# Pooled attention and a GELU MoE on one core: keys and values of batches 2 and 3 transposed through DRAM, and other chunks lent to VectorE

## Chip, cores and metric

The kernel runs on one core of a Trainium2 chip. The metric is the device time of one execution in microseconds (us); the time before is 948.67 us, the median of three runs (948.58 to 948.71).

## The reference

```python
# q: (4, 12288, 128)  kv: (4, 384, 32, 128)  w_sr: (128, 128)
# w_in: (128, 2048)   w_out: (2048, 128), all float32
kv_pool = kv.reshape(B, H // 4, 4, W // 4, 4, C).mean(axis=(2, 4))   # 96 x 8 = 768 keys a batch
k = v = kv_pool.reshape(B, -1, C) @ w_sr
s = (q @ k.transpose(0, 2, 1)) / np.sqrt(C)
a = softmax(s)
x = (a @ v).reshape(B * 12288, C)
h = x @ w_in
out = (h * sigmoid(1.702 * h)) @ w_out
```

Keys and values are the same matrix; the kernel needs it in two layouts, with channels along the partitions for the scores (kT) and with keys along the partitions for the weighted sum (v).

## The kernel before, in words

The 49152 tokens are 96 groups of 512. The work has two rounds of 48 groups, and in each round first the attention of all 48 groups, then their MoE. The unit is a chunk: 128 keys (6 a group, JC) or 128 hidden columns (16 a group, FCH) by 512 tokens, one bank of PSUM.

A **fill** writes up to three chunks into three banks with one matmul each (L350 for scores, L596 for hidden columns), and one ACTIVATE turns the three into exponentials (L352) or GELUs (L598) in SBUF. The two sets of three banks alternate. A **drain** consumes a chunk: L363, four matmuls of 129 columns for attention (the 129th sums the weights), or L606, one matmul of 512 columns into the output bank of the group. Two banks are left as accumulators (acc). When a group is finished VectorE (DVE) evacuates it: L386 and L389 divide and write x, L617 transposes the MoE's output into o_sb (three buffers), and four DMAs on SP's queue store it (L619). The last group is drained differently, by 64 matmuls of 128 columns (L634).

Some chunks skip ScalarE (ACT): DVE computes their exponential (early_exp, L426) or GELU (lent_gelu, L448) with a dozen elementwise instructions. Their matmuls are L415 and L409. Early chunks are the 24 of groups 48 to 51 (in the first MoE); rolling ones are the last chunk of listed attention groups (9 of them); lent ones are the last chunk of listed MoE groups (17, all in the second round). Rolling and lent results lie in three buffers (aside); raw, a buffer out of the queries' pool, holds a lent chunk's scaled input.

The order on every engine is written when the program is built. From L793 on, a planner keeps estimates of PE's, ACT's and DVE's time in units of one matmul; it places each fill two ahead of the drains, and puts drains and side jobs (extras, early steps) between fills as long as ACT's estimated end allows. background and background_moe (L527, L556) issue what goes with a group.

The keys of batches 2 and 3 are made during the first MoE. add_kv loads the 32 slices of kv with accumulating DMAs from POOL's queue, two per group, each pair behind a gate (a DVE memset that POOL's next memset waits for, L516); sum_kv (L176) adds two halves on DVE into pooled (96 rows by 4 x 128). Then come three side jobs on PE for each half a of a batch: transpose_pooled (L181: four transposes against an identity and a DVE copy into pT), make_k (L188: one matmul of 384 columns and a copy into kT) and make_v (L195: three matmuls of 128 columns and a copy into v). For batch 2 the adds begin at MoE group 2 and the sums stand at groups 12 and 14; for batch 3 at 24, 34 and 36 (L575 to L580).

Queries and, through x_bf, the attention's output already go through DRAM: put_away stores 3072 rows of x, bring_back loads them transposed with one DMA (L509), and load_qT does the same for 2048 queries (L215). All of these stand on SP's queue with the output stores.

Of the kernel before, what the change touches and what calls it, by code (L numbers as in the profile page):

```python
# [24 lines left out]
def kernel(  # L25
# [5 lines left out]
    r = 4  # L31
# [17 lines left out]
    q_flat = q.rearrange("b n c -> (b n) c")  # L49
    x_bf = nc.dram_tensor("x_bf", (B * N, C), BF, kind="Internal").ap()  # L50
    q_bf = nc.dram_tensor("q_bf", (B * N, C), BF, kind="Internal").ap()

    kv_r = kv.rearrange("b (ch p) (a w) c -> b a ch p (w c)", p=128, a=2)

# [43 lines left out]
    def acc_bf():  # L98
        return acc().bitcast(BF)
# [20 lines left out]
    def new_keys(b):  # L120
        kTs[b] = kvres.tile([128, J], BF, name="kT")

        vs[b] = kvres.tile([128, JC, C + 8], BF, name="v")
        nc.vector.memset(vs[b][:, :, C:C + 1], 1.0)

    def load_chunk(b, jc):
# [51 lines left out]
        pooled[b, a] = kvtmp.tile([Hp, 4, C], BF, name="pooled")  # L178
        nc.vector.tensor_tensor(pooled[b, a], t[:, 0], t[:, 1], ADD)

    def transpose_pooled(b, a):  # L181
        ps = acc_bf()[:, 0:h].rearrange("p (a b) -> p a b", a=4)
        for wp in range(4):
            nc.tensor.transpose(ps[:, wp, :], pooled[b, a][:, wp, :], ident[:Hp, :Hp])
        pTs[b, a] = kvtmp.tile([128, h], BF, name="pT")
        nc.vector.tensor_copy(pTs[b, a], ps.rearrange("p a b -> p (a b)"))

    def make_k(b, a):  # L188
        ps = acc()
        if a == 0:  # L190
            new_keys(b)
        nc.tensor.matmul(ps[:, :h], w_sr_sb, pTs[b, a], start=True, stop=True)  # L192
        nc.vector.tensor_copy(kTs[b][:, a * h:(a + 1) * h], ps[:, :h])

    def make_v(b, a):  # L195
        ps = acc()
        pT = pTs.pop((b, a))
        for k in range(K):
            nc.tensor.matmul(ps[:, k * C:(k + 1) * C], pT[:, k * 128:(k + 1) * 128], w_sr_sb,
                             start=True, stop=True)  # L200
        nc.vector.tensor_copy(vs[b][:, a * K:(a + 1) * K, 0:C], ps[:, :h].rearrange("p (k c) -> p k c", k=K))
        for jc in range(a * K, a * K + K):
            vs[b, jc] = True

# [123 lines left out]
        return K * len(free_frames())  # L328

    early = range(NG // R, NG // R + EARLY)  # L330
    rolling = [(i, JC - 1) for i in [10, *range(38, NG // R, 6), *range(57, 90, 6)]]
    lent = [(g, FCH - 1) for g in range(52, 94) if g % 5 in (2, 4)]
    aside = agpool.tile([128, K, 512], BF, name="aside")

    def weights(c):
        if c[0] == "a" and c[1] in early:
            return ag[:, (c[1] - early[0]) * JC + c[2], :]
        if c[0] == "a" and c[1:] in rolling:
            return aside[:, rolling.index(c[1:]) % K, :]
        if c[0] == "m" and c[1:] in lent:  # L340
            return aside[:, (len(rolling) + lent.index(c[1:])) % K, :]
        return ag[:, slot_of[c], :]


# [56 lines left out]
    COEFFS = (1.0000001192092896, -0.6931469440460205, 0.24022120237350464, -0.05550713464617729, 0.009675541892647743, -0.001327647129073739)  # L401

    def early_fill(i, jc):
        nonlocal steps, raw
        ps = acc()
        if (i, jc) in lent:
            if raw is None:
                raw = qpool.tile([128, 1, SG], BF, name="qT")[:, 0, 0:2 * G].bitcast(F32)
# [8 lines left out]
        early_step()  # L417

    def early_step():
# [59 lines left out]
    raw = None  # L479
    made, used = {}, []  # L480
    steps, early_todo = None, [c for c in rolling if c[0] < early[0]]
    early_todo += [(i, jc) for i in early for jc in range(JC)]
    early_todo += [c for c in rolling if c[0] > early[-1]] + lent

    def early_fits(p, i, jc):
        if (i, jc) in rolling:
            group = seq[p][1][0][0] if seq[p][0] == "a" else seq[p][1][0][0] // (NG // R) * (NG // R) + NG // R - 1
            return (i // GB, jc) in vs and (i in turned or i // 4 in qTs and i // 4 - 1 <= group // 4 and i >= 4 * QS) and len(used) > rolling.index((i, jc)) - K
        if (i, jc) in lent:
            return seq[p][0] == "m" and seq[p][1][0][0] >= i - 2 and len(used) > len(rolling) + lent.index((i, jc)) - K  # L490
        return low and min(slot_of.values()) >= low and (2, JC - 1) in vs

    def early_waits(t):
# [26 lines left out]
        nc.vector.memset(one, 0.0)  # L520
        nc.gpsimd.memset(one, 0.0)  # L521

    TURN = {6: 3, 7: 4, 8: 5, 20: 6, 21: 7, 22: 8, 25: 9, 32: 10, 35: 11, 40: 12}
    CAST = {0: [5], 13: [6], 14: [7], 15: [8], 16: [9], 26: [10, 11], 27: [12]}
    CAST_MOE = {20: 13, 21: 14, 22: 15, 23: 16, 33: 17, 34: 18, 35: 19, 36: 20, 37: 21, 38: 22, 39: 23}

    def background(i):  # L527

        first_round = i < GB * 2
        s = TURN.get(i, NS) if first_round else i // 4 + 3 if i % 4 == 0 else NS  # L530
        if s < NS:
            load_qT(s)
        if i in CAST:
            gate()
            for s in CAST[i]:
                cast_q(s)
        if i in (10, 12):
            gate()
            for jc in range(i % 10 * 3 // 2, i % 10 * 3 // 2 + 3):
                load_chunk(1, jc)  # L540
        if 0 <= i - 16 < JC:
            extras.append((key_and_value, 1, i - 16))
        if 0 <= i - 15 < JC:
            extras.append((pool_chunk, 1, i - 15))
        if i in (28, 33, 38):
            put_away(0, (i - 28) // 5)
        if i in (31, 36, 41):
            bring_back(0, (i - 31) // 5)
        if i == 28:
            gate()  # L550
            nc.gpsimd.dma_start(out=w_in_sb, in_=moe_w_in)
        if i == 29:
            gate()
            nc.gpsimd.dma_start(out=w_out_sb, in_=moe_w_out.rearrange("(o p) c -> p o c", p=128))

    def background_moe(g):  # L556

        n, g = divmod(g, 4 * XS)
        m, odd = divmod(g - 9, 2)
        m += FIRST  # L560
        if n == 0 and FIRST <= m < RT // PART:
            (bring_back if odd else put_away)(n, m)
        g += n * 4 * XS
        nonlocal low
        if g == 12:
            low = EARLY * JC
            order[:] = [f for f in order if f >= low // K]
        if g in CAST_MOE:
            gate()
            cast_q(CAST_MOE[g])  # L570
        if g in (41, 42):
            load_qT(g - 28)
        if g == 43:
            background(early[0])
        for b, lo in ((2, 2), (3, 24)):  # L575
            if lo <= g < lo + 8:
                gate()
                add_kv(b, g - lo)
            if g in (lo + 10, lo + 12):
                use_kv(b, (g - lo - 10) // 2)  # L580

    def use_kv(b, a):
        nonlocal extra_at
        sum_kv(b, a)
        on_dve(3.5)
        extra_at = max(extra_at, dve + 1.5)
        extras.extend([(transpose_pooled, b, a), (make_k, b, a), (make_v, b, a)])

    extras = []

# [120 lines left out]
    def prepare(p):  # L711
# [3 lines left out]
        for i, jc in part:  # L715
# [30 lines left out]
    FIXED, CHUNK, SWITCH, HANDOVER, EVACUATE = 0.295, 1.978, 6.0, 1.0, 4.5  # L746
    COST = {pool_chunk: (1.9, 2.6), key_chunk: (0.3, 2.4), value_chunk: (0.3, 2.4),
            transpose_q: (1.05, 4.2), early_fill: (1.0, 5.5), key_and_value: (0.55, 3.5),
            transpose_pooled: (0.9, 3.6), make_k: (0.8, 3.2), make_v: (0.8, 3.7)}
# [8 lines left out]
    def on_dve(cost):  # L758
        nonlocal dve
        dve = max(dve, now + 1.0) + cost  # L760
# [36 lines left out]
    for n in range(len(seq)):  # L797
        fill(n + 2)
        jobs(n + 3)
        while True:  # L800
# [13 lines left out]
            if f:  # L814
                now = max(now, bank) + COST[f][0]
                f(*args)
                free[last_acc] = dve + 1.0 if f is early_fill else copied(f)
                if f in (transpose_pooled, make_k, make_v):
                    on_dve(2.5)
                extra_at = max(now + PAUSE, dve + 1.5 if f in (transpose_pooled, make_k, make_v) else 0.0)  # L820
# [72 lines left out]
```

## Time and profile before

| | before |
|---|---|
| median of the runs | 948.67 us |
| span of the profiled execution | 946.7 us (2.0 under the median) |
| PE busy | 933.9 us, 6200 matmuls on record, 6314 weight loads |
| ACT busy | 933.5 us |
| DVE busy | 575.1 us, 61% |
| POOL busy | 66.5 us |
| granted TensorE clock | 1.000 |
| first fill of the first MoE | about 140 us |
| first fill of the second MoE | about 603 us |

The span is the time from the first to the last instruction of one execution under the hardware profiler. PE is TensorE's matmul row and PEld its weight loads, which overlap the matmul before. Busy time counts an engine as busy while any of its instructions is open; since matmuls and ACTIVATEs overlap their neighbours, a share of 99% does not say which engine the others wait for. The times from one matmul's or load's start to the next say more, and they are used below.

### The profile page before, as it was taken

What the parts mean: (1) busy time and instruction counts of PE and PEld (TensorE: products, weight loads), DVE (VectorE), ACT (ScalarE), POOL (GpSimd) and SP (SyncE); (2) the same over time, 40 slices, a digit from 0 to 9 for tenths busy, and PEclk for the clock granted to TensorE, in tenths of its full rate; (3) what the DMA queues carried; (4) which work ended last, traced back from release to release, by engine and by line L of the source; (5) the groups of instructions that cost most, each with busy time, mean ns of one, the idle gap of its engine ahead of it and who ended that gap; (6) DMA issues with size and microseconds to landing.
All of it is one profiled execution on the core that took longest, in us unless ns stands there. A gap on an engine that the chain in (4) does not pass through costs nothing.

```text
span 946.7 us, 15374 instructions
## 1 busy us (share of the span) xinstructions
PE 933.9 (99%) x6200; PEld 502.5 (53%) x6314; DVE 575.1 (61%) x1091; ACT 933.5 (99%) x709; POOL 66.5 (7%) x115
## 2 busy tenths in 40 slices
PE   8999999999999999999999999999999999999998
PEld 4677776444444444444446777744444444444444
DVE  5753653011678776667765765376767766777651
ACT  6999999999999999999999999999999999999998
POOL 3101001330000232000000000000000000000000
PEclk9999999999999999999999999999999999999999
DMA  9997943999867799865335683552222222222222
GB/s 210 195 207 168 181 92 52 130 163 170 164 117 114 119 147 119 127 99 87 56 58 105 138 170 84 119 123 42 36 39 40 38 41 34 44 34 45 34 45 46
DMA packets 372856, 95.46 MB, mean 101 GB/s; under 512 B 346720, under 2 KB 370400, under 8 KB 372320
## 3 DMA queue, kind: packets, MB, share of 16 engines
q1 hardware_dynamic: 344000, 62.36, 36.9%
q0 software_dynamic: 28512, 31.99, 22.3%
q8 instruction: 49, 0.80, 0.3%
q14 instruction: 23, 0.19, 0.1%
q10 hardware_dynamic: 272, 0.13, 0.0%
HBM read 52.49 MB, written 48.76 MB: 107 GB/s over the span
## 4 chain that ended last, share of the span: by engine, by line
PE 97%; ACT 1%; DMA 1%; issue 1%; DVE 0%; POOL 0%; POOLq 0%
PE banks L606 35%; PE banks L596 34%; PE banks L363 14%; PE banks L350 12%; ACT ag L352 1%; PE banks L415 1%; DMA x<-in_kv_dram 1%; PE banks L139 0%; PE banks L409 0%; PE banks L634 0%; PE banks L236 0%; POOL x L222 0%; PE banks L161 0%; PE banks L294 0%; PE banks L192 0%
## 5 line engine op out<-in xcount | busy, mean ns | idle before, releaser
L598 ACT ACTIVATE ag<-banks 128x1536 bf16<-128x1536 f32 (+1 forms) x509 | 681.1, 1489 | 0.0
L596 PE MATMUL banks<-x,w_in_sb 128*128 128x512 bf16 x1476 | 405.8, 379 | 1.7
L606 PE MATMUL banks<-ag,w_out_sb 128*128 128x512 bf16 x1477 | 402.6, 379 | 1.7
L352 ACT ACTIVATE ag<-banks 128x1536 bf16<-128x1536 f32 (+2 forms) x192 | 245.6, 1421 | 3.5 <-PE banks L236 2.3
L606 PEld LDWEIGHTS <-w_out_sb 128*128 128x128 bf16 x1520 | 148.3, 98 | 177.2 <-issue 0.2
L596 PEld LDWEIGHTS <-w_in_sb 128*128 128x128 bf16 x1519 | 147.1, 98 | 171.3 <-issue 0.7
L617 DVE STREAM_TRANSPOSE o_sb<-banks 128x512 f32<-128x512 f32 x95 | 68.1, 717 | 171.4 <-PE banks L606 166.9
L363 PEld LDWEIGHTS <-ag 128*128 128x128 bf16 x2268 | 145.5, 98 | 44.6 <-issue 0.3
L363 PE MATMUL banks<-v,ag 128*128 128x129 bf16 x2268 | 163.0, 220 | 0.2
L350 PE MATMUL banks<-qT,kT 128*128 128x512 bf16 x498 | 145.0, 379 | 3.5 <-ACT ag L352 0.5
L442 DVE SCALAR_TENSOR_TENSOR ea<-ea,eb 128x512 f32<-128x512 f32 x132 | 90.4, 685 | 3.7 <-DVE ea L442 0.7
L386 DVE RECIPROCAL rec<-banks 128x3 f32<-128x3 f32 x124 | 22.3, 180 | 85.3 <-PE banks L363 84.9
L389 DVE TENSOR_TENSOR x<-banks,rec 128x384 bf16<-128x384 f32 x124 | 69.1, 557 | 4.3
L350 PEld LDWEIGHTS <-kT 128*128 128x128 bf16 x543 | 45.8, 98 | 25.9 <-issue 2.0
L473 DVE RECIPROCAL eb<-ea 128x256 f32<-128x256 f32 x34 | 57.6, 1724 | 0.5
L466 DVE SCALAR_TENSOR_TENSOR ea<-ea,eb 128x512 f32<-128x512 f32 x68 | 46.5, 683 | 1.9
L173 POOL DMA_DIRECT2D kvs<-in_kv_dram x32 | 40.4, 1323 | 19.3 <-DMA kvs<-in_kv_dram 17.1
L431 DVE TENSOR_SCALAR ea<-banks 128x512 f32<-128x512 f32 x33 | 22.8, 692 | 29.6 <-PE banks L415 29.2
L521 POOL MEMSET gate_tile<- 1x1 f32 x38 | 3.4, 89 | 325.8 <-DVE gate_tile L520 325.8
L453 DVE TENSOR_SCALAR qT<-banks 128x512 f32<-128x512 f32 x17 | 11.8, 692 | 20.7 <-PE banks L409 20.6
L437 DVE SCALAR_TENSOR_TENSOR eb<-eb,ea 128x512 f32<-128x512 f32 x33 | 22.8, 691 | 0.9
L444 DVE SCALAR_TENSOR_TENSOR ag<-ea,ee 128x512 bf16<-128x512 f32 x24 | 16.6, 691 | 1.2
(83 smaller groups left out, 286.3 us busy)
## 6 DMA issues: line engine op xcount, KB each, us to landing
out_dram<-o_sb SPq DMA_DIRECT2D x380, 64.0 KB, 2.0
kvs<-in_kv_dram POOLq DMA_DIRECT2D x32, 384.0 KB, 6.3
q_bf<-in_q_dram POOLq DMA_DIRECT2D x21, 512.0 KB, 6.6
x_bf<-x SPq DMA_DIRECT2D x13, 768.0 KB, 5.6
x<-in_kv_dram POOLq DMA_DIRECT2D x11, 512.0 KB, 10.4
x_bf<-x SPq DMA_DIRECT2D x6, 384.0 KB, 4.6
x<-in_q_dram POOLq DMA_DIRECT2D x5, 256.0 KB, 15.3
x<-in_kv_dram SPq DMA_DIRECT2D x1, 1024.0 KB, 5.0
```

Of the source, the lines that this page charges most:

```text
L173: nc.gpsimd.dma_start(out=kv_sums[b][:, i2], in_=kv_p[b, i, w, :, i2], **({"accum_op": ADD} if n else {}))
L350: nc.tensor.matmul(ps[:, k, :], kTs[i // GB][:, jc * 128:(jc + 1) * 128], rhs, start=True, stop=True)
L352: nc.scalar.activation(place([("a",) + c for c in chunks]), ps, AF.Exp, scale=scale)
L363: nc.tensor.matmul(av_of[u][:, k * (C + 1):(k + 1) * (C + 1)], weights(("a", i, jc))[:, o:o + T], vs[i // GB][:, jc, 0:C + 1], start=(jc = ...
L389: nc.vector.tensor_tensor(to, ps[:, :, 0:C], rec.unsqueeze(2).broadcast_to([128, TS, C]), MUL)
L442: nc.vector.scalar_tensor_tensor(a, a, COEFFS[k], b, ADD, MUL)
L466: nc.vector.scalar_tensor_tensor(a, a, COEFFS[k], b, ADD, MUL)
L473: nc.vector.reciprocal(b[:, m:m + 256], a[:, m:m + 256])
L596: nc.tensor.matmul(ps[:, k, :], w_in_sb[:, fc * 128:(fc + 1) * 128], x[:, g % (4 * XS) * G:(g % (4 * XS) + 1) * G], start=True, stop=True)
L598: nc.scalar.activation(place([("m",) + c for c in chunks]), ps, AF.Gelu_apprx_sigmoid)
L606: nc.tensor.matmul(o_of[g], w_out_sb[:, fc, :], weights(("m", g, fc)), start=(fc == 0), stop=(fc == FCH - 1))
L617: nc.vector.transpose(o_sb, o_of.pop(g))
```

## The change

Four things change together.

- The side jobs transpose_pooled and make_v are gone. pooled is stored to DRAM (pool_bf) and loaded back transposed into pT by a DMA; make_k is as it was; then kT's half is stored to DRAM (k_bf) and three transposing DMAs write the three chunks of v. All of these DMAs stand on SP's queue. v's rows become 144 columns wide instead of 136.
- Each step has its own group. Batch 2's adds begin at group 0 instead of 2, batch 3's still at 24. For half a, counted from the first group of the adds: the sum and its store at 9 + a, the transposing load at 11 + a, make_k at 13 + a, the store of kT at 15 + a, the loads of v at 17 + a.
- 22 GELU chunks go to DVE instead of 17, three of them (groups 5, 7, 8) in the first MoE, and 10 rolling exponentials instead of 9, at other groups. The aside buffers are handed out in one common order (turn).
- raw is taken before the first MoE (at attention group 40) and again for the second, so the load of query set 12 moves from group 40 to 42.

```diff
-        vs[b] = kvres.tile([128, JC, C + 8], BF, name="v")
+        vs[b] = kvres.tile([128, JC, C + 16], BF, name="v")
...
-    def transpose_pooled(b, a):
...
+    def put_pooled(b, a):
+        nc.sync.dma_start(out=pool_bf[b, a].rearrange("w h c -> h w c"), in_=pooled[b, a])
+
+    def turn_pooled(b, a):
+        pTs[b, a] = kvtmp.tile([128, 1, h], BF, name="pT")
+        nc.sync.dma_start_transpose(out=pTs[b, a], in_=pool_bf[b, a].rearrange("w h c -> (w h) c"))
+
+    def put_k(b, a):
+        jc = slice(a * K, a * K + K)
+        nc.sync.dma_start(out=k_bf[b, jc].rearrange("j c t -> c j t"),
+                          in_=kTs[b][:, a * h:(a + 1) * h].rearrange("c (j t) -> c j t", t=128))
+
+    def turn_k(b, a):
+        for jc in range(a * K, a * K + K):
+            nc.sync.dma_start_transpose(out=vs[b][:, jc:jc + 1, 0:C], in_=k_bf[b, jc])
...
-    def make_v(b, a):
...
-    rolling = [(i, JC - 1) for i in [10, *range(38, NG // R, 6), *range(57, 90, 6)]]
-    lent = [(g, FCH - 1) for g in range(52, 94) if g % 5 in (2, 4)]
+    rolling = [(i, JC - 1) for i in (11, 29, 39, 42, 53, 55, 61, 73, 76, 89)]
+    lent = [(g, FCH - 1) for g in (5, 7, 8, 52, 54, 56, 57, 61, 62, 65, 68, 70, 72, 75, 77, 79, 81, 83, 86, 89, 92, 94)]
...
-    TURN = {6: 3, 7: 4, 8: 5, 20: 6, 21: 7, 22: 8, 25: 9, 32: 10, 35: 11, 40: 12}
+    TURN = {6: 3, 7: 4, 8: 5, 20: 6, 21: 7, 22: 8, 25: 9, 32: 10, 35: 11, 42: 12}
...
+        if i == 40:
+            new_raw()
...
         if g == 43:
+            raw = None
             background(early[0])
-        for b, lo in ((2, 2), (3, 24)):
+        for b, lo in ((2, 0), (3, 24)):
             if lo <= g < lo + 8:
                 gate()
                 add_kv(b, g - lo)
-            if g in (lo + 10, lo + 12):
-                use_kv(b, (g - lo - 10) // 2)
...
+            for a in range(2):
+                step = g - lo - 9 - a
+                if step == 0:
+                    sum_kv(b, a)
+                    on_dve(3.5)
+                    put_pooled(b, a)
+                if step == 2:
+                    turn_pooled(b, a)
+                if step == 4:
+                    extras.append((make_k, b, a))
+                if step == 6:
+                    put_k(b, a)
+                if step == 8:
+                    turn_k(b, a)
```

In the built programs PE has 16 transposes (L184), 12 value matmuls (L199) and their weight loads less and is otherwise equal in number; DVE has 8 copies less and the instructions of five GELUs and one exponential more; SP has 24 DMAs more; ACT has 499 GELUs of 1536 columns instead of 501, one more of 512, and one exponential of 1536 columns turned into one of 1024.

More of the change, by code (lines that the diff above doesn't have):

```diff
@@ L51 @@
     q_bf = nc.dram_tensor("q_bf", (B * N, C), BF, kind="Internal").ap()
+    pool_bf = nc.dram_tensor("pool_bf", (B, 2, r, Hp, C), BF, kind="Internal").ap()
+    k_bf = nc.dram_tensor("k_bf", (B, JC, C, 128), BF, kind="Internal").ap()
     kv_r = kv.rearrange("b (ch p) (a w) c -> b a ch p (w c)", p=128, a=2)
@@ L179, in sum_kv @@
         nc.vector.tensor_tensor(pooled[b, a], t[:, 0], t[:, 1], ADD)
-    def transpose_pooled(b, a):
[L182 to L186, printed above, removed]
+    def put_pooled(b, a):
[10 more added lines that the diff above has]
+            nc.sync.dma_start_transpose(out=vs[b][:, jc:jc + 1, 0:C], in_=k_bf[b, jc])
     def make_k(b, a):
@@ L191, in make_k @@
             new_keys(b)
-        nc.tensor.matmul(ps[:, :h], w_sr_sb, pTs[b, a], start=True, stop=True)
+        nc.tensor.matmul(ps[:, :h], w_sr_sb, pTs.pop((b, a))[:, 0, :], start=True, stop=True)
         nc.vector.tensor_copy(kTs[b][:, a * h:(a + 1) * h], ps[:, :h])
-    def make_v(b, a):
[L196 to L201, printed above, removed]
         for jc in range(a * K, a * K + K):
@@ L330 @@
     early = range(NG // R, NG // R + EARLY)
-    rolling = [(i, JC - 1) for i in [10, *range(38, NG // R, 6), *range(57, 90, 6)]]
-    lent = [(g, FCH - 1) for g in range(52, 94) if g % 5 in (2, 4)]
+    rolling = [(i, JC - 1) for i in (11, 29, 39, 42, 53, 55, 61, 73, 76, 89)]
+    lent = [(g, FCH - 1) for g in (5, 7, 8, 52, 54, 56, 57, 61, 62, 65, 68, 70, 72, 75, 77, 79, 81, 83, 86, 89, 92, 94)]
+    turn = [("a",) + c for c in rolling if c[0] < early[0]] + [("m",) + c for c in lent if c[0] < early[0]]
+    turn += [("a",) + c for c in rolling if c[0] > early[-1]] + [("m",) + c for c in lent if c[0] > early[-1]]
     aside = agpool.tile([128, K, 512], BF, name="aside")
@@ L337, in weights @@
             return ag[:, (c[1] - early[0]) * JC + c[2], :]
[L338 to L341, printed above, removed]
+        if c in turn:
+            return aside[:, turn.index(c) % K, :]
         return ag[:, slot_of[c], :]
@@ L403, in early_fill @@
     def early_fill(i, jc):
-        nonlocal steps, raw
+        nonlocal steps
         ps = acc()
@@ L407, in early_fill @@
             if raw is None:
-                raw = qpool.tile([128, 1, SG], BF, name="qT")[:, 0, 0:2 * G].bitcast(F32)
+                new_raw()
             nc.tensor.matmul(ps, w_in_sb[:, jc * 128:(jc + 1) * 128],
@@ L417, in early_fill, with new_raw @@
         early_step()
+    def new_raw():
+        nonlocal raw
+        raw = qpool.tile([128, 1, SG], BF, name="qT")[:, 0, 0:2 * G].bitcast(F32)
     def early_step():
@@ L481 @@
     steps, early_todo = None, [c for c in rolling if c[0] < early[0]]
+    early_todo += [c for c in lent if c[0] < early[0]]
     early_todo += [(i, jc) for i in early for jc in range(JC)]
-    early_todo += [c for c in rolling if c[0] > early[-1]] + lent
+    early_todo += [c for c in rolling + lent if c[0] > early[-1]]
     def early_fits(p, i, jc):
@@ L487, in early_fits @@
             group = seq[p][1][0][0] if seq[p][0] == "a" else seq[p][1][0][0] // (NG // R) * (NG // R) + NG // R - 1
-            return (i // GB, jc) in vs and (i in turned or i // 4 in qTs and i // 4 - 1 <= group // 4 and i >= 4 * QS) and len(used) > rolling.index((i, jc)) - K
+            return (i // GB, jc) in vs and (i in turned or i // 4 in qTs and i // 4 - 1 <= group // 4 and i >= 4 * QS) and len(used) > turn.index(("a", i, jc)) - K
         if (i, jc) in lent:
-            return seq[p][0] == "m" and seq[p][1][0][0] >= i - 2 and len(used) > len(rolling) + lent.index((i, jc)) - K
+            return seq[p][0] == "m" and seq[p][1][0][0] >= i - 2 and len(used) > turn.index(("m", i, jc)) - K
         return low and min(slot_of.values()) >= low and (2, JC - 1) in vs
@@ L548, in background @@
             bring_back(0, (i - 31) // 5)
+        if i == 40:
+            new_raw()
         if i == 28:
@@ L563, in background_moe @@
         g += n * 4 * XS
-        nonlocal low
+        nonlocal low, raw
         if g == 12:
@@ L578, in background_moe @@
                 add_kv(b, g - lo)
-            if g in (lo + 10, lo + 12):
-                use_kv(b, (g - lo - 10) // 2)
[L582 to L587, printed above, removed]
+            for a in range(2):
[12 more added lines that the diff above has]
+                    turn_k(b, a)
     extras = []
@@ L748 @@
             transpose_q: (1.05, 4.2), early_fill: (1.0, 5.5), key_and_value: (0.55, 3.5),
-            transpose_pooled: (0.9, 3.6), make_k: (0.8, 3.2), make_v: (0.8, 3.7)}
+            make_k: (0.8, 3.2)}
     COPY = {pool_chunk: 1.5, key_chunk: 1.5, value_chunk: 1.5, key_and_value: 2.8, transpose_q: 3.2}
@@ L817 @@
                 free[last_acc] = dve + 1.0 if f is early_fill else copied(f)
-                if f in (transpose_pooled, make_k, make_v):
+                if f is make_k:
                     on_dve(2.5)
-                extra_at = max(now + PAUSE, dve + 1.5 if f in (transpose_pooled, make_k, make_v) else 0.0)
+                extra_at = max(now + PAUSE, dve + 1.5 if f is make_k else 0.0)
                 if f is early_fill:
```

## The prediction

> **What bounds the kernel now.** I read four views: the busy times, the chain that ended last, the groups of matmuls with their weight loads, and the timeline around the removed instructions. The page, first parts 1 and 4, then groups:
>
> ```profile
> PE 933.9 (99%) x6200; PEld 502.5 (53%) x6314; DVE 575.1 (61%) x1091; ACT 933.5 (99%) x709; POOL 66.5 (7%) x115
> ...
> PE 97%; ACT 1%; DMA 1%; issue 1%; DVE 0%; POOL 0%; POOLq 0%
> ...
> L598 ACT ACTIVATE ag<-banks 128x1536 bf16<-128x1536 f32 (+1 forms) x509 | 681.1, 1489 | 0.0
> L596 PE MATMUL banks<-x,w_in_sb 128*128 128x512 bf16 x1476 | 405.8, 379 | 1.7
> L606 PE MATMUL banks<-ag,w_out_sb 128*128 128x512 bf16 x1477 | 402.6, 379 | 1.7
> ...
> L606 PEld LDWEIGHTS <-w_out_sb 128*128 128x128 bf16 x1520 | 148.3, 98 | 177.2 <-issue 0.2
> L596 PEld LDWEIGHTS <-w_in_sb 128*128 128x128 bf16 x1519 | 147.1, 98 | 171.3 <-issue 0.7
> ```
>
> PE and ACT are both at 99%, so which of them is the bound has to be decided. The chain says PE (97%). The groups show a trap: L606 has 1520 weight loads but 1477 matmuls, so 43 matmul records are missing, and a missing one looks like a gap of 0.216 us. I therefore take the steps from one weight load's start to the next, less the width of the matmul between. PE's idle time is then 10.4 us in all: 9.0 in the first 60 us, and only 1.4 in the 883 us after them. ACT is not so tight: half of the 499 steps between GELUs of 1536 columns take 1331 ns, the mean is 1344, and each longer step (1347, 1387) ends in an ACTIVATE that starts 414 ns after the last matmul of its fill, the shortest such distance in the stretch I listed. There ACT waits for PE. **PE is the bound**, and ACT has about 0.2 us to spare in 20.
>
> Next, the removed instructions in the timeline (start, length, engine, line):
>
> ```profile
> 228.85 0.40 PEld L184 LDWEIGHTS <-pooled 96*128 96x128 bf16 x4
> 229.06 0.34 PE L184 MATMUL banks<-ident,pooled 96*128 96x96 bf16 x4
> ...
> 229.23 0.81 PE L596 MATMUL banks<-x,w_in_sb 128*128 128x512 bf16 x3
> ...
> 231.56 0.33 PE L199 MATMUL banks<-w_sr_sb,pT 128*128 128x128 bf16 x3
> 231.67 0.37 PEld L596 LDWEIGHTS <-w_in_sb 128*128 128x128 bf16 x3
> 231.72 0.81 PE L596 MATMUL banks<-x,w_in_sb 128*128 128x512 bf16 x3
> ```
>
> From 229.06 to the next fill at 229.23 the four transposes cost 0.17 us; the three value matmuls 0.16 to 0.17 (231.56 to 231.72). Nothing waits around them.
>
> **The change, part by part.**
>
> *Removed from PE:* 16 transposes at 42.5 ns apart and 12 value matmuls at 56: 0.68 + 0.67 = **-1.35 us**. All of it lies on the saturated engine. make_k's four matmuls stay.
>
> *GELU and exponentials moved to DVE.* A lent chunk's matmul only moves from L596 to L409 (or L350 to L415) and its drain stays, so PE's work is unchanged. ACT loses two 1536-column GELUs net of one new 512-column one, and a 1536-column exponential becomes a 1024-column one. By start-to-start steps (1331, 904 and 477 ns) that is 2 x 1.331 - 0.477 + 0.427 = 2.6 us, on an engine that waits for PE anyway: I cost it at nothing. It keeps ACT ahead of the lighter PE. Counting chunks filled and not yet drained in the built order, before never has under 8 between 15 and 930 us, and after has as many or more from 90 to 915 us (up to 9 more): PE always has a drain to run.
>
> DVE gains 5 GELUs of 11.05 us (sum of its 15 rows from L453 to L475, 3.45 of it the two reciprocals) and one exponential of 6.1, and loses 8 copies (4 x 0.36 + 4 x 0.56): 55.3 + 6.1 - 3.7 = 57.7, so 61% becomes 67%. Three GELUs fall in groups 3 to 9, where the trace has DVE idle 5.97 us of each 6.7. What can become late is an output's evacuation (L617) behind a 1.72 us reciprocal; the next group drains into the other accumulator bank and needs the first one a group (some 7 us) later. If that cover fails, at most 1.7 us a time. In before, gaps of 38 to 108 ns follow 7 of the 50 matmuls made for DVE (0.55 us together): six more cost 0.07.
>
> *Transposing through DRAM.* SP gains 24 DMAs: 4 puts of pooled, 4 turns of 384 rows, 4 puts of keys, 12 turns of 128 rows. No such small turn is in the trace; the nearest rows:
>
> ```profile
> out_dram<-o_sb SPq DMA_DIRECT2D x380, 64.0 KB, 2.0
> kvs<-in_kv_dram POOLq DMA_DIRECT2D x32, 384.0 KB, 6.3
> ...
> qT<-q_bf SPq DMA_TRANSPOSE x21, 4.2
> ...
> x<-x_bf SPq DMA_TRANSPOSE x16, 7.4
> ```
>
> The 21 turns of 2048 rows land in 3.8 to 8.3 us, those of 3072 in 5.0 to 17.5; issuing holds SP at least 1.64 and 2.95. By the two shortest, 1.2 us per 1024 rows, a 384-row turn lands in about 1.9 (an estimate); the far end is 8.3. I take 2 to 4, since it is smaller than the nearest row.
>
> Three waits are new. (1) make_k waits for the turned keys. For each batch the second turn writes the one pT buffer, so on SP it waits for the first make_k on PE. In the built order the second make_k stands 6.85 us of PE work later in batch 2 (6.6 in batch 3); less the first matmul and the issue, about **6.1 us** remain for landing. At 2 to 4 us that costs nothing; at 8.3 it costs 2.2 us in each of two places. (2) Behind that waiting turn on SP stand the next group's four output stores, held some 7 us; o_sb has three buffers, so an evacuation needs them three groups later, and the next x turns are for groups tens of us ahead. (3) The sums now come at groups 9 and 10 instead of 12 and 14, and batch 2's adds two groups earlier, at 0 to 7, on a POOL queue that had idled 64.8 us before them and has nothing else queued until group 20. The last pair then lands near 203 us (issued about 195, landing 5.6 to 6.7 us in that stretch before) and the sum stands near 205; if late by 2 us, DVE's next work (a GELU whose chunk is drained 10 us later, and an evacuation) takes it. The second sum also waits until the first put has left the one pooled buffer: 2.0 to 12.2 us by the rows (12.2: x's store at 207.6, beside the adds that now end earlier), with a group between. The value turns are issued at groups 17 and 18; the first early drain that reads them is at 22. The query turn moved from group 40 to 42 is first read about 100 us later.
>
> *The tail.* The last fill is now one chunk. The three matmuls that wait for group 94's evacuation (L634 into the held bank) stand 0.94 us after the last L606's start (two steps of 0.216 and nine of 0.056); in the trace that evacuation ends 1.13 us after it (938.12 to 938.53 + 0.72). **+0.2 us.** The first 835 matmuls, 67 us, stand as before, so the start's 9 us of idle stay.
>
> *Sum:* -1.35 + 0.2 + 0.07 = -1.1 us. The span of 946.7 becomes 945.6; the median of the runs lies 2.0 above the span, so 948.67 becomes **947.6**.
>
> Two rules of the Trainium skill speak against this. "VectorE: DVE Perf Modes", The three transpose paths, gives 390 ns for a 128x128 transpose on TensorE and 1309 through the DMA crossbar, and its rules say to use TensorE where PSUM will do. By it a 384-row turn is three of these, an estimate of 3.9 us, still under the 6.1 above: the same sum. The rows here show why the slower path may pay: PE's next transpose starts 42 ns later, yet PE has no other idle time to put it in. "Perfetto Trace Analysis", Identifying the Most-Contended Engine, calls matmul busy time a poor measure and uses weight-load busy time: 53% here, so PE would look half free and ACT the bound, and the gain would be ACT's 2.6. The load-to-load steps disagree; this case follows the steps.
>
> **Rivals.**
> - *ACT is the bound* and its 2.6 us come off: 946.1. For: 99% busy, half the steps at their shortest. Against: 1.4 us of PE idle in 883. Chance 0.09.
> - *PE waits for the turned keys* at make_k, at the second half of each batch, if a turn lands over 6.1 us after issue. Two landings of 8 to 8.5 us give +3.8 to +4.8: 951.4 to 952.4, slower than before by over 0.2% from about 7.7 on. For: rows up to 8.3 and 17.5, casts on the same DMA engines for batch 3. Also for: the page's DMA row shows 0.9 and 0.8 of the engines busy around batch 2's turns, 0.6 around batch 3's. Against: a fifth to an eighth of those rows' size, and batch 2's adds are over earlier. Chance 0.11.
> - *DVE is late* with evacuations or a sum, one or two reciprocals' worth seen by PE: +0.4 to +1.8, 948.0 to 949.4. Chance 0.08.
> - *Forecast:* 946.8 to 948.2, chance 0.72.
>
> The range takes the forecast and the late DVE, 946.8 to 949.4, leaving out 0.20. About 0.2% (1.9 us) is what a measurement can tell from no change; the forecast lies within it. Faster 0.09, same 0.80, slower 0.11.
>
> **What would show it.** Right: no L184 and L199 rows; PE idle by load steps still about 1.4 us after 60 us; ACT's mean step longer than 1344 or unchanged while its work is 2.6 us less; no wait of PE at make_k's L192. Wrong: a wait there for a DMA, L617 waiting for DVE with PE gaps behind it, or ACT steps at 1331 with PE gaps between fills.

## The result, and the profile after

The changed kernel takes **947.22 us** (median of 20 runs, 947.08 to 947.95), the kernel before 948.57 (20 runs beside them, 948.33 to 948.75): 1.35 us less, a ratio of 0.9987 (0.9981 to 0.9993). The forecast was 1.1 us less. The difference lies under the 0.2% that the prediction took as measurable; its interval leaves out 1. The span of the profiled execution falls from 946.7 to 945.4 us.

The page of the changed kernel, in the rows that answer to those of before (busy time, count; then the shares of the chain that ended last; then groups with busy time, mean ns and the idle time before them). Lines have moved: L612 is the fill (L596 before), L622 the drain (L606), L614 the GELU (L598), L633 the evacuation (L617), L203 make_k's matmul (L192), L650 the last group's drain (L634). The kernels of the experiments have numbers of their own, a few lines off.

```profile
PE 938.4 (99%) x6286; PEld 501.3 (53%) x6286; DVE 630.5 (67%) x1168; ACT 931.0 (98%) x708; POOL 66.8 (7%) x115
...
PE 97%; ACT 1%; DMA 1%; DVE 0%; issue 0%; POOL 0%; POOLq 0%
...
L614 ACT ACTIVATE ag<-banks 128x1536 bf16<-128x1536 f32 (+1 forms) x508 | 679.1, 1470 | 0.0
L612 PE MATMUL banks<-x,w_in_sb 128*128 128x512 bf16 x1514 | 409.6, 379 | 0.0
L622 PE MATMUL banks<-ag,w_out_sb 128*128 128x512 bf16 x1498 | 405.2, 379 | 0.0
...
L622 PEld LDWEIGHTS <-w_out_sb 128*128 128x128 bf16 x1520 | 148.6, 98 | 178.6 <-issue 0.2
```

Three things are to be read here, and one isn't. PE has 28 weight loads fewer (6314 to 6286): the 16 transposes and 12 value matmuls. ACT has 2.5 us less and DVE 55.4 more (57.7 was worked out). What isn't to be read is that PE is busy 4.5 us longer: this profile lost fewer matmul records (L612 has 1514 for its 1514 weight loads, where the fill before had 1476 for 1519), and busy time counts the records that are there.

The steps between weight loads, read as in the prediction, are not touched by that. PE's idle time after the first 60 us is 1.40 us before and 1.73 after (first 60 us: 8.96 and 8.91); its work is 1.35 us less; its last matmul ends at 943.40 and at 942.33. The level of 1.40 hangs on the width taken for a matmul: some 0.2 ns more for each makes it about 0.7. The differences between kernels, on which what follows rests, move by 0.01 with it. So -1.35 + 0.33 - 0.05 = -1.07, which is the whole shift of PE's end. The remaining 0.2 of the span lie behind it, where the last stores land (3.28 us from PE's end to the span's end before, 3.09 after).

The new idle time is in few places: 194 ns before the first fill of the first MoE (139.84), 134 ns before the fill at 405.72, 185 ns in all behind matmuls made for DVE (550 before), and 253 ns at the end. The first two are waits for ACT: the ACTIVATEs that free the banks end at 139.79 and 405.67. The last of them, in the timeline of the changed kernel (start, length, engine, line; the bracket is the idle time before and what ended it):

```profile
937.91 0.38 PE L622 MATMUL banks<-aside,w_out_sb 128*128 128x512 bf16 x1
...
938.13 0.33 PE L650 MATMUL banks<-w_out_sb,ag 128*128 128x128 bf16 x3
...
938.33 0.72 DVE L633 STREAM_TRANSPOSE o_sb<-banks 128x512 f32<-128x512 f32 x1 [5.83 <-PE banks L622]
938.51 0.86 PE L650 MATMUL banks<-w_out_sb,ag 128*128 128x128 bf16 x8
939.10 0.15 PEld L650 LDWEIGHTS <-ag 128*128 128x128 bf16 x2 [0.21 <-issue]
```

Group 94's evacuation ends at 938.33 + 0.72 = 939.05. PE has run the matmuls that don't need its bank by then (the last fill is one chunk now), and the next load starts at 939.10. That is the tail term of the prediction: 0.2 forecast, 0.25 measured.

The transfers of the changed kernel, from its DMA rows (issues, KB each, median us from issue to landing):

```profile
pool_bf<-pooled SPq DMA_DIRECT2D x4, 96.0 KB, 4.5
k_bf<-kT SPq DMA_DIRECT2D x4, 96.0 KB, 2.1
...
v<-k_bf SPq DMA_TRANSPOSE x12, 2.6
...
pT<-pool_bf SPq DMA_TRANSPOSE x4, 5.8
```

And batch 3's second turn in the timeline:

```profile
405.21 0.33 PE L203 MATMUL banks<-pT,w_sr_sb 128*128 128x384 bf16 x1
...
405.56 4.78 SPq L188 DMA_TRANSPOSE pT<-pool_bf  x1
...
411.98 0.33 PE L203 MATMUL banks<-pT,w_sr_sb 128*128 128x384 bf16 x1
```

The turn is issued when the first make_k has read pT, holds SP's queue for 4.78 us and lands 5.9 us after its issue, at 411.5: half a microsecond before the matmul that reads it. The four landings are 5.6, 2.2, 6.1 and 5.9 us; the prediction took 2 to 4. Nothing waited, but the cover was nearly used up.

### The profile page after: what moved, and what is told of

It reads as the page before. It is cut to its first block, busy times and chain, and to the rows that moved or that the text cites. A ratio compares the mean times of both kernels' runs of the same rounds, so it can differ in the third digit from the quotient of the medians.

```text
span 945.4 us, 15529 instructions
## 1 busy us (share of the span) xinstructions
PE 938.4 (99%) x6286; PEld 501.3 (53%) x6286; DVE 630.5 (67%) x1168; ACT 931.0 (98%) x708; POOL 66.8 (7%) x115
## 4 chain that ended last, share of the span: by engine, by line
PE 97%; ACT 1%; DMA 1%; DVE 0%; issue 0%; POOL 0%; POOLq 0%
PE banks L622 35%; PE banks L612 35%; PE banks L366 14%; PE banks L353 12%; ACT ag L355 1%; PE banks L418 1%; DMA x<-in_kv_dram 1%; PE banks L412 1%; PE banks L141 0%; PE banks L650 0%; POOL x L225 0%; PE banks L163 0%; PE banks L239 0%; PE banks L297 0%; DVE o_sb L633 0%
## 5 line engine op out<-in xcount | busy, mean ns | idle before, releaser
L614 ACT ACTIVATE ag<-banks 128x1536 bf16<-128x1536 f32 (+1 forms) x508 | 679.1, 1470 | 0.0
L612 PE MATMUL banks<-x,w_in_sb 128*128 128x512 bf16 x1514 | 409.6, 379 | 0.0
L622 PE MATMUL banks<-ag,w_out_sb 128*128 128x512 bf16 x1498 | 405.2, 379 | 0.0
L622 PEld LDWEIGHTS <-w_out_sb 128*128 128x128 bf16 x1520 | 148.6, 98 | 178.6 <-issue 0.2
L612 PEld LDWEIGHTS <-w_in_sb 128*128 128x128 bf16 x1514 | 146.7, 98 | 170.6 <-issue 0.6
L353 PE MATMUL banks<-qT,kT 128*128 128x512 bf16 x542 | 148.3, 379 | 1.5 <-ACT ag L355 0.5
L633 DVE STREAM_TRANSPOSE o_sb<-banks 128x512 f32<-128x512 f32 x95 | 67.7, 712 | 104.1 <-PE banks L622 101.2
L449 DVE SCALAR_TENSOR_TENSOR ea<-ea,eb 128x512 f32<-128x512 f32 x136 | 93.4, 687 | 4.0 <-DVE ea L446 0.7
L480 DVE RECIPROCAL eb<-ea 128x256 f32<-128x256 f32 x44 | 75.0, 1725 | 0.7
L473 DVE SCALAR_TENSOR_TENSOR ea<-ea,eb 128x512 f32<-128x512 f32 x88 | 60.4, 686 | 2.6
L460 DVE TENSOR_SCALAR qT<-banks 128x512 f32<-128x512 f32 x22 | 15.2, 692 | 29.5 <-PE banks L412 29.5
```

The source lines that it names most:

```text
L353: nc.tensor.matmul(ps[:, k, :], kTs[i // GB][:, jc * 128:(jc + 1) * 128], rhs, start=True, stop=True)
L449: nc.vector.scalar_tensor_tensor(a, a, COEFFS[k], b, ADD, MUL)
L473: nc.vector.scalar_tensor_tensor(a, a, COEFFS[k], b, ADD, MUL)
L480: nc.vector.reciprocal(b[:, m:m + 256], a[:, m:m + 256])
L612: nc.tensor.matmul(ps[:, k, :], w_in_sb[:, fc * 128:(fc + 1) * 128], x[:, g % (4 * XS) * G:(g % (4 * XS) + 1) * G], start=True, stop=True)
L614: nc.scalar.activation(place([("m",) + c for c in chunks]), ps, AF.Gelu_apprx_sigmoid)
```

## The experiments

Two questions were open. Does the saving come from PE alone, with the lending at no effect, as the prediction has it? The rival: **PE and ACT are level**, so that less work on PE pays only if ACT has less too (first in the plain form "ACT is the bound", later as a balance of the two). The expectations call them the PE theory, the ACT theory and the balance theory. And how far off is the wait for the turned keys? All kernels compute the whole result. Each ratio is against the kernel before, run beside it (948.44 to 948.52 us in these jobs).

### The DRAM path alone

```diff
-    rolling = [(i, JC - 1) for i in (11, 29, 39, 42, 53, 55, 61, 73, 76, 89)]
-    lent = [(g, FCH - 1) for g in (5, 7, 8, 52, 54, 56, ...)]          # 22
+    rolling = [(i, JC - 1) for i in [10, *range(38, NG // R, 6), *range(57, 90, 6)]]
+    lent = [(g, FCH - 1) for g in range(52, 94) if g % 5 in (2, 4)]      # 17, as before
```

The extra raw buffer and the move of query set 12 are undone with it.

> The transposing through DRAM alone, with the 17 GELUs and 9 exponentials of before at their old groups. PE theory (the gain is the 28 matmuls taken from PE, and lending is worth nothing): the whole gain is here, 1.35 us under before, 947.2 (947.0 to 947.4), a little under the changed kernel, since the last fill keeps two chunks and the 0.25 us wait at the end is gone. ACT theory (the gain comes from chunks taken from ACT): no gain, 948.4 to 948.7.

Measured: 948.35 us (948.04 to 948.65), 0.9998 (0.9989 to 1.0007); span 946.0. The theory that PE alone pays falls: PE has its 1.35 us less work here too, and 0.2 of it are left in the median (0.6 in the spans of the two profiled executions). PE's timeline at the end of this kernel shows who took the rest:

```profile
940.71 0.94 PE L647 MATMUL banks<-w_out_sb,ag 128*128 128x128 bf16 x14
941.99 0.96 PE L647 MATMUL banks<-w_out_sb,ag 128*128 128x128 bf16 x14 [0.33 <-ACT ag L611]
```

PE waits for the last GELU: 0.33 us by the modelled ends of the matmuls, 0.50 from start to start. Two more waits of 0.2, for an ACTIVATE of exponentials to free its banks, stand at 535.3 and 566.2. Idle time after 60 us is 2.39 us instead of 1.40.

### The lending alone

The lists, raw and batch 2's earlier adds of the change, with transpose_pooled and make_v on PE and their copies on DVE as before:

```diff
-            for a in range(2):
-                step = g - lo - 9 - a
...
+            if g in (lo + 10, lo + 12):
+                use_kv(b, (g - lo - 10) // 2)
```

> The lending alone: 22 GELUs and 10 exponentials on DVE as in the changed kernel, but keys and values of batches 2 and 3 transposed on PE as before (batch 2's adds at groups 0 to 7, sums at 10 and 12). PE theory: no gain, and PE waits about 0.4 us at the end, since the 64 last matmuls follow group 94's drain with no fill between: 948.8 to 949.1. ACT theory: 2.6 us under before, 946.0.

Measured: 949.66 us (949.53 to 949.83), 1.0012 (1.0003 to 1.0021), 1.1 us slower; ACT as the only bound would have given 946.0. PE's idle time is 2.84 us (+1.44): 0.47 at the end, where PE waits for group 94's evacuation as above; 0.16 twice around make_k of batch 2, where a drain stands until DVE has cleared columns of v (the first at 214.56; the memset, L126, ends at 214.55), and some 0.11 each behind more of DVE's matmuls (five of them here, one in the changed kernel). So -0.2 alone and +1.1 alone make -1.35 together: the two halves can't be added.

### Dead matmuls put back

To the changed kernel, ahead of each make_k, three matmuls of 128 columns and four of 96 are added, whose results are overwritten. That is the PE time of the removed instructions, without their copies.

```diff
+        for k in range(K):
+            nc.tensor.matmul(ps[:, k * C:(k + 1) * C], pT[:, 0, k * 128:(k + 1) * 128], w_sr_sb, start=True, stop=True)
+        for wp in range(4):
+            nc.tensor.matmul(ps[:, wp * 96:wp * 96 + 96], w_sr_sb, pT[:, 0, wp * 96:wp * 96 + 96], start=True, stop=True)
```

> The changed kernel with dead work: ahead of each make_k matmul PE does three matmuls of 128 columns and four of 96 into the same bank, whose results are overwritten. PE theory: 4 x (3 x 56 + 4 x 42.5) ns = 1.35 us more, 948.5 to 948.7, the time of before. If instead the copies, bank holdings and waits of the removed side jobs were what cost time: 947.2, unchanged.

Measured: 948.46 us (948.28 to 948.69), 0.9999 (0.999 to 1.0008): 1.24 more than the changed kernel; PE's end moves by 1.12. As expected: once ACT is relieved, PE's 1.35 us count nearly in full.

### Group 94's chunk given back

```diff
-    lent = [(g, FCH - 1) for g in (5, 7, 8, ..., 86, 89, 92, 94)]
+    lent = [(g, FCH - 1) for g in (5, 7, 8, ..., 86, 89, 92)]
```

> The changed kernel with the lent GELU of group 94 given back to ACT (21 lent), so that the last fill has two chunks again and stands between group 94's last drain and the matmuls that wait for its evacuation. PE theory: the wait of 0.25 us at the end goes, 947.0 (946.8 to 947.2), and PE's idle time after 60 us falls from 1.7 to about 1.5 us. ACT theory: ACT has one chunk more, 947.2 + 0.44 = 947.7.

Measured: 947.10 us (946.86 to 947.44), 0.9985 (0.9976 to 0.9994). PE's timeline has two chunks in the last fill and no wait behind it:

```profile
938.06 0.33 PE L650 MATMUL banks<-w_out_sb,ag 128*128 128x128 bf16 x3
938.25 0.59 PE L612 MATMUL banks<-x,w_in_sb 128*128 128x512 bf16 x2
938.68 1.01 PE L650 MATMUL banks<-w_out_sb,ag 128*128 128x128 bf16 x15
```

The 253 ns wait is gone (idle time 1.51 instead of 1.73), so its cause is shown. The median is 0.12 under the changed kernel's and their runs overlap, so that it is quicker isn't shown. It has the lowest median of all kernels run.

### Two buffers for the turned keys

```diff
-        pTs[b, a] = kvtmp.tile([128, 1, h], BF, name="pT")
+        pTs[b, a] = kvtmp.tile([128, 1, h], BF, name="pT", bufs=2)
```

(A small tile was put elsewhere to make room.)

> The changed kernel with two pT buffers (a small setup tile lies in the chunk buffer instead, to make room), so that the second turn of a batch no longer waits on SP for the first make_k. PE theory: PE never waited for that turn, so 947.2 (947.0 to 947.4), while the second turns are issued about 7 us ahead of the first make_k's end instead of behind it and the 0.5 us left before batch 3's second make_k becomes several us. If that wait costs time now: 0.1 to 0.5 us less.

Measured: 947.35 us (947.11 to 947.86), 0.9988 (0.9979 to 0.9997), the same as with one buffer, as expected where PE doesn't wait. What was expected of the issue was half wrong. Batch 2's second turn moved from 233.45 to 226.49; batch 3's was issued at 406.10, as late as ever: on SP's queue it stands behind eight output stores that wait for their evacuations for 14.1 us (391.91 to 406.0). There the order of the queue sets it, not the buffer.

### The second make_k close behind the first

```diff
-                if step == 4:
+                if step == 4 - a:
                     extras.append((make_k, b, a))
```

The single buffer stays, so the second matmul must wait for the whole round trip.

> The changed kernel with the second make_k of each batch one group earlier, 1.2 us (batch 2) and 1.5 us (batch 3) behind the first, while its turned keys are still ordered only once the first is done. Price of the wait that the forecast's rival named: with the landings of the changed kernel's trace (2.2 and 5.9 us after issue) PE waits 1.3 and 4.8 us, and 0.2 more at the end, 953.4; with two landings of 2.2, 950.5. If PE has other work to hide it: 947.2 to 947.5.

Measured: 955.28 us (954.85 to 956.26), 1.0074 (1.0061 to 1.0087): 8.06 more than the changed kernel, about 2 more than was expected. PE waits 1.49 us before the matmul at 235.91 and 4.04 before the one at 412.19 (from start to start, less the width of the matmul between). The second wait in PE's timeline, and stretches of PE, PEld, DVE, ACT and POOL busy time behind it (then granted clock, DMA share, GB/s):

```profile
407.93 0.38 PE L622 MATMUL banks<-ag,w_out_sb 128*128 128x512 bf16 x1
412.19 0.34 PE L203 MATMUL banks<-pT,w_sr_sb 128*128 128x384 bf16 x1 [3.88 <-DMA pT<-pool_bf]
```

```profile
412.00:413.00 1.00, 0.81 (x4) 0.41 (x5) 0.44 (x1) 0.00 (x0) 0.00 (x0) 1.00 0.72 124
413.00:414.00 1.00, 1.00 (x11) 0.82 (x10) 0.97 (x3) 0.79 (x1) 0.00 (x0) 0.70 0.68 116
414.00:415.00 1.00, 1.00 (x9) 0.72 (x7) 0.18 (x1) 0.66 (x1) 0.00 (x0) 0.50 0.68 116
415.00:416.00 1.00, 1.00 (x5) 0.44 (x4) 0.00 (x0) 0.00 (x0) 0.00 (x0) 0.50 0.68 116
416.00:417.00 1.00, 1.00 (x14) 1.00 (x12) 0.55 (x2) 0.91 (x1) 0.00 (x0) 0.59 0.32 53
417.00:420.00 3.00, 2.95 (x23) 1.69 (x22) 2.37 (x7) 2.64 (x3) 0.53 (x2) 1.00 0.00 0
```

The clock goes from 1.00 to 0.50 behind the long wait and is back at 417: 0.30 + 0.50 + 0.50 + 0.41 = 1.71 us lost in these four rows, which is 3.4 us at half clock. With the waits and 0.2 more at the end, 1.49 + 4.04 + 1.71 + 0.2 = 7.4 of the measured 8.06; the rest lies in gaps of under 0.2 us each (8.0 in all by the steps). After the wait of 1.49 us the clock stayed at 1.00. So the wait that the prediction feared is dear where the cover is missing; in the changed kernel it is covered with half a microsecond to spare. That the turned keys land slowly because casting loads run beside them wasn't tried.

### No GELU lent, and half of them

```diff
-    lent = [(g, FCH - 1) for g in (5, 7, 8, 52, 54, 56, ...)]   # 22
+    lent = [(g, FCH - 1) for g in ()]                           # none
```

and, in a second kernel, 11: (5, 8, 54, 57, 62, 68, 72, 77, 81, 86, 92).

> The changed kernel with no GELU lent to DVE (22 chunks back on ACT, 22 x 0.444 = 9.8 us of its work). PE theory: ACT has about 9 us of waits for PE to give up and a lead of some 20 chunks, so the time rises by much less than 9.8: 947.2 to 950.5. ACT theory: 957.0.

> The changed kernel with 11 GELUs lent instead of 22 (4.9 us of work back on ACT; the last fill has two chunks). PE theory: ACT still has time to spare, 947.0 to 947.4. ACT theory: 952.1.

Measured: none 954.76 us (954.69 to 954.79), 1.0066 (1.0053 to 1.0079); half 950.69 (950.44 to 951.43), 1.0024 (1.0015 to 1.0033). Both lie between the theories. PE's timeline without lending, at 800 us:

```profile
800.88 0.81 PE L612 MATMUL banks<-x,w_in_sb 128*128 128x512 bf16 x3
801.52 0.81 PE L622 MATMUL banks<-ag,w_out_sb 128*128 128x512 bf16 x3
802.22 0.81 PE L612 MATMUL banks<-x,w_in_sb 128*128 128x512 bf16 x3
802.86 0.81 PE L622 MATMUL banks<-ag,w_out_sb 128*128 128x512 bf16 x3
803.56 0.81 PE L612 MATMUL banks<-x,w_in_sb 128*128 128x512 bf16 x3
```

Fills start every 1.34 us (800.88, 802.22, 803.56), and six matmuls of 0.2157 take 1.294: PE waits 0.05 in each step. ACT is what it waits for (the ACTIVATE that frees the banks of the fill at 802.22 ends at 802.17), and ACT's own step here is 1.342 to 1.344, not 1.331, since each ACTIVATE in turn starts 418 ns after the start of its fill's last matmul. About 1.343 us is therefore the pace at which the two go round even where ACT holds PE up, and ACT's mean step in the kernel before (1344.1 ns; 1343.4 without lending) is hardly longer. **ACT had next to no slack there.** A chunk costs it 1.344 / 3 = 0.448 us. Eleven chunks given back are 4.93 us and cost 3.47, so ACT was 1.5 us ahead in the changed kernel. By all 22 (9.86 us, which cost 7.54) it would be 2.3; why the second eleven cost less isn't shown.

The ends of the traces tell the same. From the start of the last ACTIVATE to PE's last end it takes 2.03 us in the DRAM path alone and in the half lending, where PE waits for ACT at the end; 2.36 in before and 3.47 after. So ACT was 0.3 us ahead in before and 1.4 after. (The last ACTIVATE of the changed kernel has one chunk instead of two and is 0.42 us shorter; counted from its end the lead is 1.9.)

### The kernel before with fewer and more lent chunks

If the two are level in before, giving ACT three chunks back must cost at once, and taking three off can't help, since PE keeps its work:

```diff
-    lent = [(g, FCH - 1) for g in range(52, 94) if g % 5 in (2, 4)]                       # 17
+    lent = [(g, FCH - 1) for g in (52, 54, 59, 62, 64, 67, 69, 74, 77, 79, 82, 84, 89, 92)]  # 14
```

> The kernel before with 14 lent GELUs instead of 17. The theory that the runs so far suggest (balance theory: PE and ACT both bind; a chunk that ACT gets back costs its 0.448 us step once ACT's lead over PE is used up, and before has little lead left, since its last ACTIVATE ends about 0.4 us ahead of the matmul that needs it): 3 x 0.448 - 0.4 = 0.9 us more, 949.4 (949.1 to 949.8). The forecast's theory (PE alone binds, ACT has time to spare): 948.5, unchanged.

Measured: 949.27 us (949.19 to 949.43), 1.0009 (1.0 to 1.0018). The balance gives 3 x 0.448 - 0.3 = 1.0; measured 0.83 in the median, 1.02 in idle time, 0.80 of it one wait for ACT at the end. No run of the one overlaps with one of the other, so the forecast's view (no change) falls.

With 20 in the second round (55, 70 and 85 added to the 17):

> The kernel before with 20 lent GELUs instead of 17; its fills end well ahead of its drains. Balance theory: ACT's lead grows and PE's work stays, so no gain, 948.5, and 0.4 us more for the wait for group 94's evacuation at the end: 948.5 to 949.1. ACT theory: 3 x 0.448 = 1.3 us less, 947.2.

Measured: 956.97 us (956.84 to 957.04), 1.009 (1.0076 to 1.0104), which neither theory had; idle time 9.88 us, in runs of two or three waits of some 0.7 us between fills. The next but one kernel shows why.

### The DRAM path with three more chunks lent

The first experiment's kernel, with the GELUs of groups 5, 7 and 8 on DVE (and for them raw and the later load of query set 12, as in the change):

```diff
-    lent = [(g, FCH - 1) for g in range(52, 94) if g % 5 in (2, 4)]
+    lent = [(g, FCH - 1) for g in (5, 7, 8, *range(52, 94)) if g < 48 or g % 5 in (2, 4)]
```

> The transposing through DRAM with the 17 GELUs and 9 exponentials of before, and three GELUs more in the first MoE (groups 5, 7, 8): 20 lent. Balance theory: ACT has three chunks (1.34 us) more than in the changed kernel, which by the run with 11 lent (3.4 us slower for 4.9 us of work) has about 1.5 us of lead to give up, so the gain is whole again: 947.2 (947.0 to 947.6), 1.1 under the run without the three. The forecast's theory: no difference from that run, 948.3.

Measured: 947.43 us (947.02 to 948.61), 0.999 (0.9981 to 0.9999). Three chunks of relief for ACT bring 0.9 of the 1.1 us by which the first experiment missed the change (2 of the 11 runs lie in the range of that one). Idle time is 1.72, with the wait for ACT at the end gone.

### One more lent than in the change

```diff
-    lent = [(g, FCH - 1) for g in (5, 7, 8, 52, 54, 56, 57, 61, 62, 65, 68, ..., 92, 94)]      # 22
+    lent = [(g, FCH - 1) for g in (5, 7, 8, 52, 54, 56, 57, 59, 61, 62, 65, 66, 68, ..., 92)]  # 23
```

Group 94's chunk is given back, and those of 59 and 66 are lent.

> The changed kernel with 23 GELUs lent (20 of them in the second round). Balance theory: PE binds, so nothing more is to be had: 947.2 to 947.5, the 0.2 being a longer wait for group 94's evacuation at the end, since no fill is left to stand between. ACT theory: 0.45 us less, 946.8.

Measured: 958.76 us (958.68 to 958.95), 1.0109 (1.0095 to 1.0123), against every expectation: 11.54 more than the changed kernel, and PE's idle time is 11.55 more. PE's timeline of this kernel at 714 us:

```profile
714.08 0.81 PE L612 MATMUL banks<-x,w_in_sb 128*128 128x512 bf16 x3
715.24 0.81 PE L612 MATMUL banks<-x,w_in_sb 128*128 128x512 bf16 x3 [0.35 <-ACT ag L614]
716.59 0.81 PE L612 MATMUL banks<-x,w_in_sb 128*128 128x512 bf16 x3 [0.54 <-ACT ag L614]
```

Fill follows fill with no drain between (there is no L622), and each waits about 0.7 us for ACT to free a set of banks. The reader sees a wait for ACT, but ACT isn't the cause: the written order holds no drains there. The planner starts a group's drains only when its lent chunk should be ready (L841 of before), and with 20 lent in the second round its estimate of DVE is behind. In this kernel's plan that rule holds the drains back at 25 fills, ten of them in a row for group 62. The trace has no drain from 713.9 to 726.8, though DVE finishes that group's chunk at 720.9. The drains come later, when there is no fill to run beside them. In the plan of before with 20 the rule acts at 19 fills; in those of before (17 there) and of the change (19) at none.

## Why the prediction was right in its sum, and where it failed

The sum was near (-1.1 forecast, -1.35 measured), and most terms behind it were; one reason was not, and there was luck in the sum.

- **PE's removed work, -1.35.** Right, and shown by the dead matmuls (+1.24).
- **The tail, +0.2.** Right: 0.25 measured, and gone where group 94's chunk is given back, though the median then moves by no more than can be told.
- **Gaps behind DVE's matmuls, +0.07.** Wrong in sign: 0.55 us became 0.19. Two waits that it didn't name, both for ACT, 0.19 at the first MoE's first fill and 0.13 at 405.72, take their place. Idle time in all rose by 0.33 where 0.27 was the sum of the two terms, so the total came out by errors that cancelled.
- **The step that failed: lending, "I cost it at nothing", on an engine with "about 0.2 us to spare in 20".** Without it most of the 1.35 can't be had: the DRAM path alone is 1.13 us above the whole change, and the same working, PE's work alone, would have forecast -1.35 for it. The prediction does say that lending "keeps ACT ahead of the lighter PE", but it puts no price on that. So it was luck, as far as the reasons go, that the change had enough lending in it. The reading behind the step was that ACT's 1331 ns step is its pace and that 1344 means waiting for PE. Without lending ACT is the one waited for, and its step is 1342 to 1344. The waits of ACT for PE and of PE for ACT are then parts of one loop of two bank sets, and no slack. Nor does each longer step in the trace of before end in a wait for the last matmul, as the prediction read: about half do (some 75, at 412 to 416 ns), but some 80 steps of 1347 or 1348 end in an ACTIVATE 468 ns after it. The count of at least eight chunks filled and not drained was no cover either: it was made up to 930 us, and the lead runs out behind that, with the last GELU.
- **ACT as the bound** was wrong as a rival too: lending alone is 1.1 us slower, since it leaves PE's work as it was and adds waits for DVE. Neither engine alone was the bound: in before ACT was 0.3 us ahead of PE.
- **The turned keys.** "At 2 to 4 us that costs nothing": the cost was right and the size wrong (2.2 to 6.1 us). Of the room of 6.1, 0.5 us was left in batch 3. A wait of 4.04 us costs 1.7 more in clock, which the rival's price left out; whether its waits of 1.9 to 2.4 us would have cost that too isn't shown, since they lie between the 1.49 that didn't and the 4.04 that did.
- **Sums, output stores, value turns** came as worked out: batch 2's sums stand at 204.4 and 210.0, the 12 value turns land in 2.3 to 4.2 us, and no PE wait follows from any of them.

One rule of the Trainium skill bears on the clock drop. In the run with the close make_k a wait of 4.04 us was followed by a granted clock of 0.50 for 3.4 us, one of 1.49 by none. "TensorE: Matmul & The Clock Gate", Part 1: The HAM clock gate, says that the clock is halved after an idle window of about 3.4 us and restored after as long a busy one, in windows that run freely. Both waits agree with it.

Of the two rules that the prediction weighed, the one on weight-load busy time was told in part: the page names, beside it, the share of the peak rate that the matmuls reach. PE here was at work in all but some 10 us of its 943, so that measure would not have made it look half free.

Open stays why the DRAM path alone has 0.2 us to show in the median of the times but 0.5 in the median of the spans of the same runs (946.2 against 946.7), how large ACT's lead in the changed kernel is (1.4 to 2.3 us by the readings above), and whether 21 lent chunks are better than 22.

## What to carry to other kernels

Where two engines that feed each other are both at 99%, taking work off one pays only as far as the other is ahead: read that lead at the end of the trace, as the time from the second engine's last instruction to the first one's end against a run where it is waited for (with a last instruction of the same size). The pace of an engine is the step that it makes where others wait for it, and not its shortest step; giving it more work in an experiment shows that step. Before a transfer through DRAM takes the place of an on-chip step, compare the spare time of its last reader with landings measured in that very stretch, and see what stands ahead of it in its queue: behind waiting stores, a second buffer changed nothing in batch 3.

## What the runs showed of the hardware

- Small transposing DMAs are slow to land and to issue. In the changed kernel 384 rows (96 KB) took 2.2 to 6.1 us and held SP's queue 1.1 to 4.8 us, 128 rows 2.3 to 4.2 and 1.2 to 2.8. By size, from the rows of 2048 and 3072, 1.9 us had been estimated for 384.
- With two sets of three banks, PE and ACT wait for each other in one step. Where no GELU was lent, an ACTIVATE starts 418 ns after the start of its fill's last matmul, the next fill of those banks starts 0.05 us after its end, and the loop settles at 1.342 to 1.344 us, although 1.331 appears in more than half of the steps of before.
- In the run with the close make_k, PE was idle for 4.04 us until 412.19, and its granted clock was 0.50 for 3.4 us, from 413.4 to 416.8; after 1.49 us of idle time it stayed at 1.00.
- A waiting output store holds the DMAs behind it on SP's queue: eight of them held it for 14.1 us, and the turn behind them was issued at 406.10 though its buffer was free.
